# Reciprocals of attention denominators on 12 values a row, between two 32x32 block transpositions on VectorE

## The chip, the core and the metric

One core of a Trainium2 chip runs the whole program. It has TensorE (PE in the rows), VectorE (DVE), ScalarE (ACT), GpSimd (POOL) and SyncE (SP), and 16 DMA engines; each compute engine works off its own queue of instructions in order, and they meet at semaphores. The metric is the device time of one execution in microseconds (us).

## The reference

Three parts follow each other on 2304 tokens (4 batches of 576). The first is a linear attention with 8 heads of 64, whose result is divided, per token and head, by a denominator; the second a gated MLP (512 to 1536 to 512) behind an RMS norm; the third a soft mixture of 8 experts with 4 slots each. The change touches the division in the first part only.

```python
    q_p, k_p = (phi(q), phi(k))              # 256 features: exp(proj), exp(-proj)
    kv = np.einsum('bhsf,bhsd->bhfd', k_p, v)
    z = np.sum(k_p, axis=2)
    num = np.einsum('bhsf,bhfd->bhsd', q_p, kv)
    den = np.einsum('bhsf,bhf->bhs', q_p, z)[..., None] + 1e-06
    return (num / den).astype(np.float32)
    ...
    rms = np.sqrt(np.mean(x * x, axis=-1, keepdims=True) + 1e-06)
    xn = x / rms * rms_g
    g = xn @ w_gate
    silu = g * (1.0 / (1.0 + np.exp(-g)))
    return (silu * (xn @ w_val) @ w_out).astype(np.float32)
```

## The kernel before

The tokens are cut into 6 blocks of 384. The program has three stages, one behind the other in the text, but each engine's order of instructions is laid down when the program is built, by a planner that estimates when each operand is ready and prefers what stands earlier in the text; so work of neighbouring steps is interleaved.

The first stage (0 to 128 us of the trace) walks over 18 tiles of 128 tokens of k and v. In each iteration i it loads k for tile i+4 and v for tile i+2, projects k (L394), takes the largest magnitude and subtracts it (L398, L402 on VectorE), takes two exponentials (L415, L416 on ScalarE) and accumulates kv and z in PSUM (L439, L448). Beside that run the weights of the MLP, which come in 1 MB pieces and are converted in steps on ScalarE (L127, L129, L102), VectorE (the join, L137, L139) and GpSimd (L105), and the q side of block 0. The second stage (128 to 676 us) runs the MLP over the blocks 0 to 5: per block 12 steps m, in each the gate and value products (L806), an activation (L813, L814, L818), a split of the result in two parts (L102, L105) and the output products (L831 to L833). Beside block b of the MLP runs the q side of block b+1. The rest is the mixture's experts.

The q side of a block is four calls of attend(c), one for each pair of heads. Blocks 0 and 1 are of class Turned (features by projection, transposition and exponential, L339), blocks 2 to 5 of class Reduced (features by a maximum over partitions on GpSimd, L280). When the steps run is written out by hand: the lists TURNED0, TURNED1 and REDUCED give for each step the number of a slot; in block 0 two slots make one iteration i (3.5 us on average), in the MLP each m has three (2 to 3 us each).

attend(c) multiplies the features e of two heads with kv into num (L206, PSUM, 128 rows of head and dimension by 384 tokens) and with z into den (L214). For den the weight is one column spread to 32, so that each 32 rows of den hold the same denominators: rows 64*hh + 32*g to that + 31 hold head hh for the tokens of half g (192 each). ScalarE copies num out of PSUM (L216). VectorE adds 1e-6 to den (L218), takes reciprocals of all 128 x 192 (L219), and ScalarE spreads them by eight copies of 32 x 192 (L224) into the layout of num: rows of a head, both halves of the tokens. VectorE multiplies (L225), ScalarE squares (L228, L231), VectorE sums the squares of the four calls in s (L232). dn, the spread reciprocals and the squares are written into the e tiles, which come free with the last of them. After the call c = 3, scale() sums s over partitions on TensorE (ssq, L241), takes the inverse root on VectorE, and out() applies it (L254); then the block's values are split for the MLP (xnh, xnl). At the end of attend(3) of blocks 1 and 2, SP loads kv of a later batch (L236).

All loads are issued by SP, in one queue: k (raw, L385) and v (vt, L411), 256 KB each; weights (wraw, L123), 1 MB; q (qraw, L262 and L317), 192 KB; kv, 520 KB.

## Time and profile before

| | us |
|---|---|
| median of 3 runs | 742.65 (741.85 to 742.89) |
| span of the profiled execution, first to last instruction | 735.0 |
| median less that span | 7.65 |
| TensorE busy | 710.2 (97%) |
| VectorE busy | 429.5 (58%) |
| ScalarE busy | 371.8 (51%) |

Each row of a trace names the source line, the engine, the operation, the tile written and the tiles read with their shapes, how often, the busy time and the mean of one, and the idle time of that engine just before with the instruction that ended it. PEld is TensorE's loading of weights, which runs beside its products. Busy times of TensorE overlap a little, since its products are pipelined.

### The profile page before, as it was taken

To read this page: it belongs to the slowest core of one execution; us is meant where nothing else is said; L and a number is where in the kernel's file an instruction comes from. 1 tells how busy PE (TensorE), PEld (TensorE's weight loads), DVE (VectorE), ACT (ScalarE), POOL (GpSimd) and SP (SyncE) were. 2 spreads that over 40 slices of the span, in tenths; PEclk is the share of its full clock that TensorE was granted. 3 is DMA by queue.
4 is the path that set the end of the run, shared out by engine and by line. 5 is a ranking of instruction groups with operands and counts; after the bars stand their busy time and mean duration, and the time that the engine had idled before them with its cause. 6 is when DMAs were issued, how large, how long until landed. Compare 5 with 4: busy or idle time off the path is not lost.

```text
span 735.0 us, 12347 instructions
## 1 busy us (share of the span) xinstructions
PE 710.2 (97%) x4919; PEld 575.0 (78%) x4919; DVE 429.5 (58%) x808; ACT 371.8 (51%) x805; POOL 107.9 (15%) x60
## 2 busy tenths in 40 slices
PE   7998999999999999999999999999999999999895
PEld 4655555988889888898888989889888899988443
DVE  5998956798746556455565555655556453423313
ACT  6899855688445555345553456534465331211103
POOL 0232200234200211011210211201211010000100
PEclk9999999999999999999999999999999999999999
DMA  9683312544011010100010010000100137657898
GB/s 321 252 289 123 88 30 102 176 162 172 0 62 33 22 26 29 38 11 22 23 31 12 1 33 22 23 20 0 33 1 2 66 139 262 228 203 284 324 365 293
DMA packets 25145, 79.45 MB, mean 108 GB/s; under 512 B 2688, under 2 KB 13376, under 8 KB 18688
## 3 DMA queue, kind: packets, MB, share of 16 engines
q1 hardware_dynamic: 24864, 77.79, 30.2%
q10 hardware_dynamic: 224, 0.88, 0.4%
q8 instruction: 38, 0.62, 0.3%
q14 instruction: 19, 0.16, 0.1%
HBM read 71.99 MB, written 6.67 MB: 107 GB/s over the span
## 4 chain that ended last, share of the span: by engine, by line
PE 79%; DVE 9%; ACT 7%; issue 2%; POOL 1%; DMA 1%; SPq 0%; DVEq 0%; ACTq 0%; POOLq 0%
PE pv L806 20%; PE pg L806 19%; PE acc L831 6%; PE acc L832 6%; PE acc L833 6%; PE num L206 4%; PE kacc L439 2%; PE den L214 2%; ACT e L224 2%; PE y L945 2%; DVE wt L139 2%; PE y L961 2%; DVE wt L137 2%; PE P L394 1%; PE kacc L448 1%
## 5 line engine op out<-in xcount | busy, mean ns | idle before, releaser
L806 PE MATMUL pv<-xnh,wv 128*128 128x384 f32 x576 | 151.5, 344 | 0.0
L806 PE MATMUL pg<-xnh,wg 128*128 128x384 f32 x576 | 150.2, 342 | 0.6 <-DVE t L814 0.4
L806 PEld LDWEIGHTS pg<-xnh,wg 128*128 128x128 f32 x576 | 104.7, 188 | 6.3 <-ACT xnh L102 0.6
L806 PEld LDWEIGHTS pv<-xnh,wv 128*128 128x128 f32 x576 | 103.2, 188 | 7.0 <-issue 6.7
L806 PE MATMUL pv<-xnl,wv 128*128 128x384 f32 x288 | 97.7, 339 | 0.0
L806 PE MATMUL pg<-xnl,wg 128*128 128x384 f32 x288 | 97.5, 338 | 0.0
L831 PE MATMUL acc<-wo,hh 128*128 128x512 f32 x216 | 88.6, 410 | 0.0
L280 POOL PARTITION_ALL_REDUCE qe<-qe x32 | 50.0, 1563 | 262.5 <-ACT qe L279 242.8
L832 PE MATMUL acc<-wo,hh 128*128 128x512 f32 x216 | 85.8, 397 | 0.0
L833 PE MATMUL acc<-wo,hl 128*128 128x512 f32 x216 | 85.4, 396 | 0.0
L102 ACT CAST hh<-t 128x384 fp32r<-128x384 f32 x72 | 36.7, 510 | 80.6 <-PE acc L832 66.1
L105 DVE TENSOR_TENSOR hl<-t,hh 128x384 fp32r<-128x384 f32 x72 | 41.3, 574 | 51.2 <-ACT hh L102 48.6
L814 DVE SCALAR_TENSOR_TENSOR t<-t,pg 128x384 f32<-128x384 f32 x72 | 39.7, 551 | 51.8 <-ACT t L813 51.7
L813 ACT ACTIVATE t<-pg 128x384 f32<-128x384 f32 x72 | 35.2, 489 | 63.8 <-PE pg L806 63.7
L224 ACT COPY qe<-qe 32x192 f32<-32x192 f32 x128 | 44.8, 350 | 31.7 <-DVE qe L219 30.4
L818 DVE TENSOR_TENSOR t<-t,pv 128x384 f32<-128x384 f32 x72 | 39.7, 552 | 30.4 <-PE pv L806 29.3
L806 PEld LDWEIGHTS pg<-xnl,wg 128*128 128x128 f32 x288 | 54.0, 188 | 0.3 <-DVE xnl L105 0.3
L806 PEld LDWEIGHTS pv<-xnl,wv 128*128 128x128 f32 x288 | 54.1, 188 | 0.1
L833 PEld LDWEIGHTS acc<-wo,hl 128*128 128x128 f32 x216 | 40.6, 188 | 10.0 <-DVE hl L105 0.3
L831 PEld LDWEIGHTS acc<-wo,hh 128*128 128x128 f32 x216 | 40.7, 189 | 7.3 <-issue 0.3
L439 PE MATMUL kacc<-kp,vt 128*64 128x256 f32 (+1 forms) x320 | 44.8, 396 | 1.7 <-ACT kp L416 1.7
L832 PEld LDWEIGHTS acc<-wo,hh 128*128 128x128 f32 x216 | 40.7, 188 | 6.4
(187 smaller groups left out, 1065.5 us busy)
## 6 DMA issues: line engine op xcount, KB each, us to landing
eu<-in_w_dram SPq DMA_DIRECT2D x32, 1024.0 KB, 6.3
wraw<-in_wg_dram SPq DMA_DIRECT2D x6, 1024.0 KB, 5.0
wraw<-in_wv_dram SPq DMA_DIRECT2D x6, 1024.0 KB, 5.2
wraw<-in_wo_dram SPq DMA_DIRECT2D x6, 1024.0 KB, 4.8
qraw<-in_qT_dram SPq DMA_DIRECT2D x32, 192.0 KB, 2.3
raw<-in_kT_dram SPq DMA_DIRECT2D x18, 256.0 KB, 4.2
vt<-in_v_dram SPq DMA_DIRECT2D x18, 256.0 KB, 4.0
out_dram<-ob SPq DMA_DIRECT2D x18, 256.0 KB, 2.8
```

What stands on the lines that cost most here:

```text
L102: ACT.copy(out=hi, in_=src)
L105: (lo_eng or POOL).tensor_tensor(out=lo, in0=src, in1=hi.bitcast(F32), op=ALU.subtract)
L224: ACT.copy(out=rd[64 * hh + 32 * r:64 * hh + 32 * r + 32, g], in_=dn[o:o + 32])
L280: POOL.partition_all_reduce(e[:, 0], e[:, 1], channels=128, reduce_op=bass_isa.ReduceOp.absmax)
L439: PE.matmul(out=kva[o0:o0 + 64, hh // 2], lhsT=self.vt[r0:r1, h], rhs=kp[r0:r1, hh].rearrange("p s f -> p (s f)"), start=first and hh < 2, ...
L806: PE.matmul(out=p, lhsT=w[:, a, c], rhs=x, start=n == 0, stop=n == 11)
L813: ACT.activation(out=t, in_=g, func=AF.Tanh, scale=0.5)
L814: DVE.scalar_tensor_tensor(out=t, in0=t, scalar=1.0, in1=g, op0=ALU.add, op1=ALU.mult)
L818: DVE.tensor_tensor(out=t, in0=t, in1=wide("v", m, xs), op=ALU.mult)
L831: PE.matmul(out=acc[i], lhsT=hh[:, s], rhs=w[:, 0], start=m == 0, stop=False)
L832: PE.matmul(out=acc[i], lhsT=hh[:, s], rhs=w[:, 1], start=False, stop=False)
L833: PE.matmul(out=acc[i], lhsT=hl[:, s], rhs=w[:, 0], start=False, stop=m == MF - 1)
```

## The change

The reciprocals are taken on fewer values. Since each 32 rows of den hold the same 192 denominators, a transposition of 32x32 blocks by VectorE puts them one to a row: dt has, in row 32*q + j and block b, the denominator of token 32*b + j of that quarter, 32 times over; only its first column is used. rw gets these 6 values a row with 1e-6 added, in both of its two halves, and their reciprocals (12 values a row). Four transfers of 32 rows x 6 values (24 bytes a row), issued by SP, carry each quarter's values to the other quarter of the same head. A new step norm(c) then transposes rw, each value read 32 times, into rd (128 x 384), which is the layout of num, and multiplies; the squares and the sum s follow as before, with the squares in rd. The eight copies by ScalarE are gone, and the e tiles are last read by the products of den.

norm(c) is a step of its own in the lists: one slot behind attend(c) in blocks 0 and 1, two behind in blocks 2 to 5. The load of kv goes to a function next_kv(), called at the end of attend(3), behind the four transfers in the text. Three small tiles are new: dt (one buffer), rw (two), rd (one).

```diff
--- before.py
+++ after.py
@@ -189,7 +189,7 @@
 
         def __init__(self, sp, ps, blk, bufs):
             self.sp, self.ps, self.blk, self.bufs = sp, ps, blk, bufs
-            self.raw, self.x, self.e = {}, {}, {}
+            self.raw, self.x, self.e, self.rw = {}, {}, {}, {}
 
         def psum(self, name, shape):
             return self.ps.tile(shape, F32, tag="misc", name=name, bufs=self.bufs["misc"])
@@ -214,24 +214,37 @@
                     PE.matmul(out=den[o:o + 32], lhsT=kvt[b][:, 2 * c + hh, s, HD:HD + 1].to_broadcast([128, 32]),
                               rhs=e[hh][:, s, t:t + BLK // 2], start=s == 0, stop=s == 1, skip_group_check=True)
             ACT.copy(out=y, in_=num)
-            dn = e[0][:, 0, 0:BLK // 2]
-            DVE.tensor_scalar(out=dn, in0=den, scalar1=1e-6, scalar2=None, op0=ALU.add)
-            DVE.reciprocal(out=dn, in_=dn)
-            rd = e[1][:, 0].rearrange("p (g t) -> p g t", g=2)
+            nb = BLK // 64
+            dt = self.sp.tile([128, nb, 32], F32, tag="dt", name="dt", bufs=1)
+            DVE.transpose(out=dt.rearrange("p b j -> p (b j)"), in_=den)
+            self.rw[c] = rw = self.sp.tile([128, 2, nb], F32, tag="rw", name="rw", bufs=2)
+            DVE.tensor_scalar(out=rw, in0=dt[:, :, 0].rearrange("p (o b) -> p o b", o=1).to_broadcast([128, 2, nb]),
+                              scalar1=1e-6, scalar2=None, op0=ALU.add)
+            DVE.reciprocal(out=rw, in_=rw)
             for hh, g in halves:
                 o = 64 * hh + 32 * g
-                for r in range(2):
-                    ACT.copy(out=rd[64 * hh + 32 * r:64 * hh + 32 * r + 32, g], in_=dn[o:o + 32])
-            DVE.tensor_tensor(out=y, in0=y, in1=e[1][:, 0], op=ALU.mult)
+                to = 64 * hh + 32 * (1 - g)
+                SP.dma_start(out=rw[to:to + 32, g], in_=rw[o:o + 32, g])
+            if c == 3:
+                self.next_kv()
+
+        def norm(self, c):
+
+            y = xraw[self.blk][:, c]
+            rd = self.sp.tile([128, BLK], F32, tag="rd", name="rd", bufs=1)
+            rw = self.rw.pop(c).rearrange("p g (b o) -> p (g b) o", o=1)
+            DVE.transpose(out=rd.rearrange("p (b j) -> p b j", j=32), in_=rw.to_broadcast([128, BLK // 32, 32]))
+            DVE.tensor_tensor(out=y, in0=y, in1=rd, op=ALU.mult)
             if c == 0:
                 self.s = self.sp.tile([128, BLK], F32, tag="s", name="s", bufs=1)
                 ACT.activation(out=self.s, in_=y, func=AF.Square)
             else:
-                sq = e[1][:, 1]
-                ACT.activation(out=sq, in_=y, func=AF.Square)
-                DVE.tensor_tensor(out=self.s, in0=self.s, in1=sq, op=ALU.add)
+                ACT.activation(out=rd, in_=y, func=AF.Square)
+                DVE.tensor_tensor(out=self.s, in0=self.s, in1=rd, op=ALU.add)
+
+        def next_kv(self):
             for b, t0, t1 in block_parts(self.blk):
-                if c == 3 and self.blk * BLK + t1 == (b + 1) * SEQ and b + 2 < NB:
+                if self.blk * BLK + t1 == (b + 1) * SEQ and b + 2 < NB:
                     kvt[b + 2] = kvp.tile([128, NH, 2, HD + 1], F32, tag="kv", name=f"kv{b + 2}", bufs=2)
                     SP.dma_start(out=kvt[b + 2].rearrange("p h s d -> p (h s d)"), in_=kv_d[b + 2])
 
@@ -306,7 +319,8 @@
             a = [lambda c=c: self.attend(c) for c in range(4)]
             g = [lambda h=h: self.exps(h) for h in range(NH)]
             s = [first, *(x for c in range(4) for x in (f[2 * c], f[2 * c + 1], g[2 * c], g[2 * c + 1], a[c])), self.scale, self.out]
-            return sorted(zip(REDUCED, s), key=lambda x: x[0])
+            s = list(zip(REDUCED, s)) + [(REDUCED[5 * c + 5] + 2, lambda c=c: self.norm(c)) for c in range(4)]
+            return sorted(s, key=lambda x: x[0])
 
     class Turned(Q):
 
@@ -364,6 +378,7 @@
                     r.append((at[c] + i, lambda c=c, i=i: p(c, i)))
                     r.append((at[c] + i + lag, lambda c=c, i=i: self.turn(c, i, pr[c, i])))
                 r.append((attend[c], lambda c=c: self.attend(c)))
+                r.append((attend[c] + 1, lambda c=c: self.norm(c)))
             r += [(end[0], self.scale), (end[1], self.out)]
             return sorted(r, key=lambda x: x[0])
```

## Rows read from the trace of the kernel before

**Rows 1.** Busy time of each engine over the span (share) xinstructions, page, part 1

```profile
PE 710.2 (97%) x4919; PEld 575.0 (78%) x4919; DVE 429.5 (58%) x808; ACT 371.8 (51%) x805; POOL 107.9 (15%) x60
```

**Rows 2.** Stages: length, then busy us of each engine, granted TensorE clock, DMA share, GB/s

```profile
52.00:92.00 40.00, 37.12 (x369) 21.36 (x362) 35.84 (x53) 35.68 (x75) 11.86 (x5) 0.96 0.39 126
92.00:128.00 36.00, 34.85 (x345) 20.16 (x344) 21.74 (x49) 19.99 (x47) 0.00 (x0) 1.00 0.20 68
128.00:229.00 101.00, 98.62 (x597) 87.14 (x597) 75.64 (x122) 65.43 (x125) 23.07 (x9) 1.00 0.30 106
229.00:676.00 447.00, 445.86 (x2686) 392.75 (x2685) 235.19 (x473) 197.09 (x464) 60.06 (x36) 1.00 0.18 61
```

**Rows 3.** The same for the copies of L224 alone: ScalarE busy, count

```profile
52.00:92.00 40.00, 8.36 (x24) 0.96 0.39 126
128.00:229.00 101.00, 11.19 (x32) 1.00 0.30 106
229.00:676.00 447.00, 44.79 (x128) 1.00 0.18 61
```

**Rows 4.** Groups by line, 52 to 92 us: busy, mean ns | idle before, releaser

```profile
L224 ACT COPY e<-e 32x192 f32<-32x192 f32 x24 | 8.4, 348 | 1.6 <-DVE e L219 1.3
...
L219 DVE RECIPROCAL e<-e 128x192 f32<-128x192 f32 x3 | 4.0, 1350 | 0.1
...
L225 DVE TENSOR_TENSOR xraw<-xraw,e 128x384 f32<-128x384 f32 x3 | 1.7, 558 | 3.5 <-ACT e L224 3.5
...
L218 DVE TENSOR_SCALAR e<-den 128x192 f32<-128x192 f32 x3 | 1.0, 346 | 0.0
```

**Rows 5.** Waits of TensorE, 52 to 92 us: total us, times, longest

```profile
PE P L322 <- ACT xraw L216: 1.9, 1, 1.9
```

**Rows 6.** Lines 680 and 681, the mixture's own denominators: ns min/median/max

```profile
L680 DVE TENSOR_SCALAR cs<-cs x6: 168/168/169, 274.9 to 689.4; 128x3 f32<-128x3 f32 x6
...
L681 DVE RECIPROCAL cs<-cs x6: 176/176/176, 275.1 to 689.6; 128x3 f32<-128x3 f32 x6
```

**Rows 7.** SP's queue around the first call: start us, us, what

```profile
57.11 0.33 SPq L123 DMA_DIRECT2D wraw<-in_wo_dram  x1
57.53 0.38 SPq L385 DMA_DIRECT2D raw<-in_kT_dram  x1
58.48 0.33 SPq L411 DMA_DIRECT2D vt<-in_v_dram  x1
```

**Rows 8.** DMA issues, 0 to 20 us: KB each, median us to landing

```profile
wbd_f<-in_wbd_dram SPq DMA_DIRECT2D x1, 128.0 KB, 2.1
...
small<-in_rmsg_dram SPq DMA_DIRECT2D x1, 2.0 KB, 3.9
```

**Rows 9.** DMA issues, whole span

```profile
qraw<-in_qT_dram SPq DMA_DIRECT2D x32, 192.0 KB, 2.3
...
kv<-kv_d SPq DMA_DIRECT2D x2, 520.0 KB, 3.5
```

**Rows 10.** Waits of TensorE, 128 to 229 us, then 229 to 676 us

```profile
PE num L206 <- ACT e L339: 1.2, 1, 1.2
PE ssq L241 <- DVE s L232: 0.7, 1, 0.7
...
PE ssq L241 <- DVE s L232: 1.1, 4, 0.3
```

**Rows 11.** Timeline, VectorE and TensorE, end of block 2's q side

```profile
299.01 0.36 DVE L218 TENSOR_SCALAR qe<-den 128x192 f32<-128x192 f32 x1 [1.18 <-PE den L214]
...
304.26 0.56 DVE L225 TENSOR_TENSOR xraw<-xraw,qe 128x384 f32<-128x384 f32 x1 [2.15 <-ACT qe L224]
...
305.41 0.56 DVE L232 TENSOR_TENSOR s<-s,qe 128x384 f32<-128x384 f32 x1
...
306.02 0.83 PE L241 MATMUL ssq<-small,s 128*128 128x1 f32 x6 [0.29 <-DVE s L232]
```

**Rows 12.** SP's queue at the same place

```profile
299.00 0.33 SPq L236 DMA_DIRECT2D kv<-kv_d  x1
```

## The prediction, made before the change was run

> **What bounds the kernel now.** I read first the busy time of each engine over the span, then the same by stage, then the waits of the stages that leave an engine room. TensorE is busy for 710.2 of 735.0 us [rows 1], so a change on other engines is worth only what TensorE waits for them. The stages say where that is [rows 2]. From 229 to 676 us, where 16 of the 24 calls of attend() lie (blocks 2 to 5), TensorE is busy 445.86 of 447.00 us: nothing that leaves ScalarE there can shorten it by more than 1.1 us. From 128 to 229 us (block 1, 4 calls) it is busy 98.62 of 101.00 us: at most 2.4 us. From 92 to 128 us it is busy 34.85 of 36.00 us: at most 1.2 us. The stage with room is 52 to 92 us, with the first three calls of block 0: TensorE 37.12 of 40.00 us at a mean granted clock of 0.96, VectorE 35.84, ScalarE 35.68, all three near full and waiting for each other. TensorE's room there is 2.9 us of idle time and about 1.6 us (0.04 x 40) of clock, 4.5 us together.
>
> Next, what ScalarE does in that stage: 8.36 of its 35.68 us are the 24 spreading copies of L224 [rows 3]. They stall the others in two ways. VectorE waits 3.5 us for them at L225, of 4.2 us that it is idle in all [rows 4]; and the copy that empties num (L216) stands behind them on ScalarE, so that TensorE waits 1.9 us for a PSUM buffer [rows 5]. So the copies are on the path in this stage and beside the path everywhere else.
>
> **The change part by part.** Removed per call: eight copies on ScalarE, mean 348 ns, 2.9 us with their issue; on VectorE one addition over 192 columns (346 ns) and one reciprocal over 192 columns (1350 ns) [rows 4]. Added on VectorE: a transposition of 128x192 out of PSUM, an addition and a reciprocal over 12 columns, a transposition into 128x384; added on SP: four transfers of 32 x 24 bytes.
>
> The small ones have near rows: over 3 columns the same two operations took 168 and 176 ns [rows 6]. By the slope of the reciprocal, (1350 - 176) / 189 = 6.2 ns a column, 12 columns take 0.23 us; the addition 0.18 us. No row shows VectorE's transposition. Bounds: from nothing beyond a pass of the same size (L218 reads 128x192 of PSUM in 0.35 us, L225 passes 128x384 in 0.56 us [rows 4]) to twice that, if each element is handled twice; nothing in the trace makes it cheaper than a plain pass. I take the plain pass, 0.35 and 0.56 us, because both are one read and one write of those sizes. VectorE per call then: removed 0.35 + 1.35 = 1.70, added 0.35 + 0.18 + 0.23 + 0.56 = 1.32, so 0.4 us less; at the dear end 1.7 + 0.5, so 0.5 us more.
>
> The Trainium skill ("VectorE: DVE Perf Modes", "The three transpose paths") gives 311 ns for VectorE's transposition of 128x128 bf16, in 32x32 blocks; with one column a cycle of 0.96 GHz beyond that, an estimate from that page is 0.38 and 0.58 us, 0.05 us a call above the plain pass, some 0.2 us over the four calls of block 0, so 738.9 us in place of the forecast below. No row of before shows it.
>
> The transfers: SP issues two in a row 0.42 us apart (57.11, 57.53) [rows 7]; four take 1.3 us up to the last issue. How long so small a one takes no row shows in this stage. Nearest: 2 KB landed 3.9 us after issue between large loads, 128 KB 2.1 us as the first load of the program [rows 8], 192 KB 2.3 us in the median of the later stages [rows 9]. I take 2.2 us on a quiet queue and 3.9 us beside loads; a much lower end has no row, but a gain from it is only an earlier start of norm(), which waits for its slot anyway. From the end of the reciprocal to the end of the normalising product: now 2.9 + 0.6 = 3.5 us; after 1.3 + 2.2 + 0.56 + 0.56 = 4.6 us quiet, 6.3 us beside loads. But the reciprocal ends earlier by 1.70 - 0.76 = 0.94 us. So the product ends 0.2 us (quiet) to 1.9 us (beside loads) later than now.
>
> Whom the lateness meets: norm() is moved one slot (blocks 0 and 1) or two (2 to 5) behind attend(), 3.5 to 4 us of other VectorE work, so its transposition should mostly find the transfers landed, and the 3.5 us of stall at L225 should go. What is late next is VectorE itself and the weight join (L137, L139) on it. Behind the four transfers on SP stand loads of k, v and weights two iterations (18 of them fill 128 us, so 14 us) ahead of use; they wait for the reciprocal some microseconds longer, and I cost that at nothing; if that lead is gone, each call costs the landing of a load, about the 3.9 us of [rows 8]. The e tiles come free after the den matmuls instead of after L232; the trace shows nobody waiting for them.
>
> Sum by stage. 52 to 92 us: VectorE's floor is 40.0 - 4.2 - 3 x 0.4 = 34.6 us and TensorE's 35.5 us, so at most 4.5 us; the first call (57 us) issues behind a 1 MB and two 256 KB loads [rows 7], and its wait may even grow. I take 3.0 us (bounds -1 and 4.5). 92 to 128 us: the fourth call's sums end 0.2 us later, and TensorE idles 1.2 us in all: 0 (-1 to 1.2). 128 to 229 us: TensorE's two longest waits are 1.2 us for an exponential (ACT e L339) and 0.7 us for s at ssq [rows 10]; the first should go: 1.0 us (-2 to 2.4). 229 to 676 us: at each block's end TensorE already waits 0.3 us at the ssq matmuls, four times [rows 10]: in block 2 den's addition starts at 299.01, the product ends at 304.8, s is ready at 306.0 and ssq starts then [rows 11]. Quiet, this moves by +0.2 us: 0 in all (-4 to 1.1). Rest of the program: 0. Total 3.0 + 1.0 = 4.0 us less: span 731.0. The profiled span of 735.0 us lies 7.65 us below the median of the runs, 742.65; with that unchanged, 738.7 us.
>
> **The rivals.** First: ScalarE was only one of three full engines. VectorE at 34.6 of 40 us, in an order laid down before the run, takes the stall back elsewhere; or the transpositions cost twice. Then 52 to 92 us gives 0.5 us and the rest nothing: 742.1 us. For it: VectorE and TensorE are 90 and 93% busy there. Against: the 1.9 and 3.5 us waits name ScalarE.
>
> Second, slower: the transfers come late and TensorE waits at each block's end for s. The place is ssq (L241), in blocks 1 to 5. SP issues in block 1 and 2 also a load of kv, 520 KB, 3.5 us to landing [rows 9], that needs only the den matmuls (299.00 us [rows 12]) and so can get in front of the four transfers; then they land like the 2 KB among loads, and s comes 1.9 us later. Five ends x 1.9 = 9.5 us, less the 4.0: 748.2 us if at all five; with 1.9 at the two with kv and 0.5 at the other three, 5.3 less 4.0, 744.0 us. It decides from 0.8 us of lateness a block on (5 x 0.8 = 4.0). For it: TensorE has no margin at ssq. Against: three of the five ends have DMA nearly idle (0.18 mean share [rows 2]), and the order of ssq on TensorE can be later than now.
> The Trainium skill ("DMA: Bandwidth & Descriptors", "Queues, rings and completion order") says that each DMA engine consumes what one issuing engine queued in ring order, which speaks for this rival: a small transfer does not pass SP's load. [...] The 3.9 us for 2 KB agree.
>
> Third, better: every wait goes, 4.5 + 1.2 + 2.4 + 1.1 = 9.2 us: 733.5 us. Against it, VectorE's floor.
>
> **How the numbers follow.** Forecast 0.50 (736.5 to 741), first rival 0.22, second 0.16, third 0.12. About 0.2%, 1.5 us, is what a measurement of this kernel can tell from no change, so "same" is 741.2 to 744.1. Faster: 0.50 + 0.12, less 0.02 of the forecast's slow edge, 0.60. Same: 0.22 + 0.02 = 0.24. Slower: 0.16. The range reaches from 733.5 (third rival) to 745.5, which holds the second rival where only some block ends are late; out of it are its dear half and the bounds taken all at once. Predicted is the forecast's 738.7.
>
> **What would show it.** Right: L224 gone; ScalarE's busy time 64 us less over the three stages of [rows 3]; VectorE's idle time ahead of norm()'s transposition under 1.5 us in 52 to 92 us; TensorE's wait for L216 gone and its clock there at 1.00; the first gate matmul of block 0, which now starts as the third stage of [rows 2] begins, 2 to 4 us earlier; block length from 229 us on unchanged. Wrong: the four transfers landing over 3 us after issue with VectorE idle before norm(); ssq waiting over 0.8 us in each block; transpositions over 0.7 us; or that matmul no earlier, with VectorE's idle time merely moved.

## The result and the profile after

The changed kernel took 744.03 us (median of 13 runs) beside 741.87 us for the kernel before (13 runs): ratio 1.0053, 95% interval 1.0027 to 1.0078. The ratio goes by the means, 745.00 and 741.09 us; the two medians alone would give 1.0029. Measured a second time, it was 1.0058 (1.0036 to 1.0080). So it is 0.5% slower, 3.9 us in the means; 738.7 us and "faster" were predicted. Ratios are of fast runs; one execution of no_transfers_edge (1396 us) was slow and is left out.

The profiled execution spans 741.2 us, 6.2 more than that of before, and that is more than the change cost. Wherever the time and the span of an execution are both on record, the time is 1.7 to 3.5 us above the span. The trace of before, with 735.0 us, is therefore of one of its fastest executions: other spans of that kernel go from 734.9 to 742.1 us, with medians of 737.4 to 738.6 on three chips.

Busy time over the span, and the stages (length, then busy us of TensorE, weight loads, VectorE, ScalarE, GpSimd, granted clock, DMA share, GB/s), beside [rows 1, 2]:

```profile
PE 714.1 (96%) x4919; PEld 574.7 (78%) x4919; DVE 428.5 (58%) x856; ACT 304.4 (41%) x613; POOL 108.9 (15%) x60
```

```profile
52.00:92.00 40.00, 36.03 (x328) 20.68 (x326) 33.57 (x50) 26.92 (x48) 12.18 (x5) 0.91 0.37 117
92.00:128.00 36.00, 35.03 (x366) 19.96 (x368) 24.69 (x58) 16.47 (x35) 0.00 (x0) 1.00 0.21 70
128.00:229.00 101.00, 97.19 (x601) 84.50 (x592) 75.60 (x125) 53.09 (x93) 21.84 (x9) 1.00 0.31 109
229.00:676.00 447.00, 446.66 (x2684) 391.41 (x2683) 232.42 (x511) 153.81 (x340) 61.87 (x36) 1.00 0.17 59
```

The copies [rows 3, 4] are gone and ScalarE has 67.4 us less to do. VectorE has nearly as much as before (428.5 against 429.5). The granted clock of 52 to 92 us, which was to rise from 0.96 to 1.00, fell to 0.91.

The new operations of VectorE (count, then busy us, mean ns, idle before and its releaser):

```profile
L236 DVE STREAM_TRANSPOSE rd<-rw 128x384 f32<-128x384 f32 x24 | 13.8, 575 | 17.9 <-DMA rw<-rw 17.9
L237 DVE TENSOR_TENSOR xraw<-xraw,rd 128x384 f32<-128x384 f32 x24 | 13.6, 566 | 0.9
L219 DVE STREAM_TRANSPOSE dt<-den 128x192 f32<-128x192 f32 x24 | 9.1, 380 | 23.6 <-PE den L214 23.6
L221 DVE TENSOR_SCALAR rw<-dt 128x12 f32<-128x12 f32 x24 | 6.1, 254 | 0.6
L223 DVE RECIPROCAL rw<-rw 128x12 f32<-128x12 f32 x24 | 5.4, 226 | 0.7
```

The four operations that replace the addition and the reciprocal sum to 34.4 us (L236, L219, L221, L223); the two old ones took 24 x (0.35 + 1.35) = 40.8. The 6.4 us saved were taken back by others: the subtraction hl<-t,hh (L105, 72 times) rose from 41.3 to 46.6 us in all, since three of them, beside a subtraction on GpSimd, took 2.4 to 2.8 us in place of 0.56, and the sum s (18 times) rose from 10.0 to 14.3.

The transfers: from issue to landing (KB each, median us), then the time that SP takes to issue one (ns min/median/max):

```profile
rw<-rw SPq DMA_DIRECT2D x96, 0.8 KB, 1.7
```

```profile
L227 SPq DMA_DIRECT2D rw<-rw x96: 507/583/1350, 59.2 to 587.0; - x96
```

TensorE's waits, 52 to 92 us and then 128 to 229 us (total, times, longest), beside [rows 5, 10]: the wait for the copy of num, 1.9 before, grew, and new ones stand in the MLP's first block.

```profile
PE P L336 <- ACT xraw L216: 2.7, 1, 2.7
...
PE acc L848 <- DVE hl L105: 1.8, 2, 1.0
PE pg L821 <- DVE t L829: 1.7, 1, 1.7
```

**Where the 6.2 us between the two traces lie.** Three marks in each trace cut the program: the first gate product of the MLP, the first copy of block 1's outputs (L869, L884 after), two blocks on, and that of block 4's, three whole blocks later. "Tail" is from there to the end of the span.

| us | first gate product | from there to outputs of block 1 | three blocks | tail | span | ratio to before (95%) |
|---|---|---|---|---|---|---|
| before | 128.05 | 194.46 | 279.99 | 132.5 | 735.0 | 1 |
| after | 130.78 | 196.21 | 280.30 | 133.9 | 741.2 | 1.0053 (1.0027–1.0078) |
| after_again | 134.22 | 196.23 | 280.30 | 133.6 | 744.3 | 1.0058 (1.0036–1.0080) |
| copies_out | 133.54 | 194.40 | 278.35 | 133.0 | 739.3 | 1.0071 (1.0044–1.0099) |
| copies_out_h13 | 132.02 | 196.10 | 278.35 | 133.0 | 739.5 | 1.0055 (1.0033–1.0077) |
| copies_back | 131.07 | 197.67 | 280.64 | 136.8 | 746.2 | 1.0062 (1.0036–1.0088) |
| copies_kept | 127.54 | 197.97 | 278.43 | 135.6 | 739.5 | 1.0049 (1.0031–1.0068) |
| no_transfers | 126.45 | 194.13 | 278.34 | 136.3 | 735.2 | 0.9976 (0.9956–0.9996) |
| no_transfers_h13 | 129.63 | 194.11 | 278.34 | 136.9 | 739.0 | 0.9972 (0.9951–0.9993) |
| no_transfers_edge | 126.24 | 194.27 | 278.34 | 132.8 | 731.6 | 0.9944 (0.9924–0.9964) |
| held13 | 126.13 | 195.78 | 280.49 | 132.9 | 735.3 | 1.0001 (0.9977–1.0025) |
| held13_join | 127.32 | 194.50 | 280.45 | 135.5 | 737.8 | 1.0001 (0.9986–1.0016) |
| two_queues | 132.04 | 195.98 | 279.12 | 132.5 | 739.6 | 1.0055 (1.0033–1.0077) |
| held13_2q | 126.83 | 195.97 | 279.65 | 132.6 | 735.0 | 0.9990 (0.9968–1.0012) |
| join_2q | 132.51 | 193.89 | 279.09 | 134.1 | 739.6 | 1.0024 (1.0000–1.0047) |
| held13_join_2q | 126.47 | 193.91 | 279.09 | 132.5 | 732.0 | 0.9961 (0.9942–0.9981) |
| all_three_again | 126.56 | 193.93 | 279.11 | 132.4 | 732.0 | 0.9963 (0.9938–0.9988) |
| before_join | 133.56 | 194.16 | 280.02 | 132.5 | 740.2 | 1.0008 (0.9992–1.0023) |

After against before: +2.7 up to the MLP, +1.8 in its first two blocks, +0.3 in the three blocks, +1.4 in the tail. Two warnings on reading this. The middle columns repeat within 0.02 us where one kernel was traced twice (after and after_again; no_transfers and no_transfers_h13); the first column moves by 3.4 us between after and after_again, and by 5.5 us between before and before_join, whose order is the same up to that mark (128.05 and 133.56), because TensorE's waits and its clock differ from one execution to the next. So whether after lies behind before there is not shown by these two traces: the 3.9 us in the means, less the 2.1 of the two middle columns, leave an estimate of 1.8 us for the first column and the tail together. And the tail has two lengths: 132.4 to 133.6 us, or 133.9 to 136.9 where the clock falls near 690 us. So the middle columns may be read from one trace; the first column and the tail need several traces and the ratios beside them.

### The profile page after: what moved, and what is told of

Read it like the earlier page. It is cut to its first block, busy times and chain, and to the rows that moved or that the text cites. A ratio compares the mean times of both kernels' runs of the same rounds, so it can differ in the third digit from the quotient of the medians.

```text
span 741.2 us, 12309 instructions
## 1 busy us (share of the span) xinstructions
PE 714.1 (96%) x4919; PEld 574.7 (78%) x4919; DVE 428.5 (58%) x856; ACT 304.4 (41%) x613; POOL 108.9 (15%) x60
## 4 chain that ended last, share of the span: by engine, by line
PE 82%; DVE 9%; ACT 3%; DMA 2%; issue 1%; POOL 1%; SPq 0%; DVEq 0%; ACTq 0%
PE pv L821 19%; PE pg L821 18%; PE acc L848 6%; PE acc L846 6%; PE acc L847 6%; PE num L206 4%; PE kacc L454 4%; DVE wt L137 3%; PE den L214 2%; PE y L960 2%; PE P L409 2%; PE kacc L463 2%; DVE wt L139 2%; PE y L976 2%; DMA wraw<-in_wg_dram 1%
## 5 line engine op out<-in xcount | busy, mean ns | idle before, releaser
L105 DVE TENSOR_TENSOR hl<-t,hh 128x384 fp32r<-128x384 f32 x72 | 46.6, 647 | 58.0 <-ACT hh L102 53.1
L829 DVE SCALAR_TENSOR_TENSOR t<-t,pg 128x384 f32<-128x384 f32 x72 | 39.6, 551 | 48.2 <-ACT t L828 48.2
L298 ACT ACTIVATE qe<-qe 128x384 f32<-128x384 f32 x32 | 16.8, 526 | 49.9 <-DVE qe L297 49.9
```

The lines of the kernel that those rows point to most:

```text
L105: (lo_eng or POOL).tensor_tensor(out=lo, in0=src, in1=hi.bitcast(F32), op=ALU.subtract)
L829: DVE.scalar_tensor_tensor(out=t, in0=t, scalar=1.0, in1=g, op0=ALU.add, op1=ALU.mult)
```

## The experiments

### What is the relief of ScalarE worth by itself?

copies_out is the kernel before without the eight copies (the product reads the reciprocals in place, so the division is left out in part). copies_back is the changed kernel with eight copies that nobody reads.

```diff
-                for r in range(2):
-                    ACT.copy(out=rd[64 * hh + 32 * r:64 * hh + 32 * r + 32, g], in_=dn[o:o + 32])
-            DVE.tensor_tensor(out=y, in0=y, in1=e[1][:, 0], op=ALU.mult)
+            DVE.tensor_tensor(out=y, in0=y, in1=e[0][:, 0], op=ALU.mult)
```

> The kernel before, with the eight spreading copies of L224 left out and nothing in their place (the product at L225 takes its second factor from the tile of the reciprocals, so the division is wrong; all else is as before, the long reciprocals too). It shows what ScalarE's freed 67 us are worth by themselves. Order theory (what the copies' going changes is the order that the planner lays down, and ScalarE's new idle time goes into waits for GpSimd and for weight loads): within 2 us of the kernel before, 740 to 744 us, and 52 to 92 us no shorter by more than 1 us. Transfer theory (the relief is worth the 3 to 5 us that the prediction gave it, and the four transfers with their waits eat it): 737 to 739 us.

> The changed kernel with the eight copies of 32x192 put back on ScalarE behind the first transposition, into the tile where they went before; nobody reads them. If ScalarE's time were worth anything, this would be 3 us or more slower than the changed kernel, 747 us or more. Order theory: the planner sorts the weight steps behind the copies again, as in the kernel before, and the time is the changed kernel's or better, 741 to 745 us, with TensorE's wait for the num copy under 2 us.

Less work made the kernel slower (1.0071), outside the range of either theory, and the copies put back cost the changed kernel nothing that the ratios can tell (1.0062 beside 1.0053). In copies_back TensorE's wait for the copy of num is gone, as the order theory had it, but TensorE waits 3.3 us for another result of ScalarE (kvs) in its place, and the column to block 1's outputs is 1.5 us longer. So no gain from freeing ScalarE shows in the first 130 us. Each of the two edits also gives a new order, so the price of ScalarE's time at a fixed order is not shown. And copies_out's three blocks are 1.64 us shorter than those of before, 0.55 us a block: there the relief does shorten the path, where the prediction expected nothing.

### One edge of order

When the program is built, the planner lays down each engine's order. What it did with the freed time of ScalarE, from 57 us (start, us, engine, line, and in brackets the idle time before with its releaser), and the product of TensorE that waits:

```profile
57.39 1.05 ACT L102 CAST wo<-wt 128x1024 fp32r<-128x1024 f32 x1 [0.59 <-DVE wt L139]
58.35 1.20 ACT L129 ACTIVATE wraw<-wraw 128x1024 uint32<-128x1024 uint32 x1
61.27 1.20 ACT L127 ACTIVATE wt<-wraw 128x1024 f32<-128x1024 f32 x1 [1.73 <-POOL wo L105]
...
64.44 1.05 ACT L102 CAST wg<-wt 128x1024 fp32r<-128x1024 f32 x1
65.37 0.49 ACT L216 COPY xraw<-num 128x384 f32<-128x384 f32 x1
```

```profile
65.92 1.22 PE L336 MATMUL P<-wbd_f,qraw 128*128 128x256 f32 x2 [2.66 <-ACT xraw L216]
```

The place of the copies is taken by a weight piece from a later iteration (L127 at 61.27). Its buffer comes free only with GpSimd's subtraction, so ScalarE stands still 1.73 us with the four exponentials kp and the copy of num behind it. In held13 that piece, the one of iteration 13, is issued behind the copy of num, where it stands in the kernel before:

```diff
-            ACT.copy(out=y, in_=num)
+            numcopy[self.blk, c] = ACT.copy(out=y, in_=num).ins
...
+HOLD = {13: 1}
...
+                    if i in HOLD:
+                        with tc.issue_after(numcopy[0, HOLD[i]]):
+                            conv_scale()
```

> The changed kernel with one edge of order more: the scaling of the weight piece of iteration 13 (two instructions on ScalarE) is queued behind the copy of num of attend(1) of block 0, where it stands in the kernel before; in the changed kernel it stands ahead of four exponentials and that copy, and waits 1.7 us for GpSimd. Order theory: TensorE's wait of 2.7 us before 66 us shrinks under 1 us, its clock from 64 to 76 us stays above 0.9, and the first gate matmul comes 2 to 4 us earlier than 130.8, so 740 to 742 us. Transfer theory: unchanged, 743 to 745 us.

```profile
61.06 0.63 ACT L432 ACTIVATE kp<-pr 128x512 f32<-128x512 f32 x1 [2.50 <-DVE pr L419]
...
64.09 0.47 ACT L218 COPY xraw<-num 128x384 f32<-128x384 f32 x1
64.46 1.16 ACT L128 ACTIVATE wt<-wraw 128x1024 f32<-128x1024 f32 x1
```

The copy of num comes 1.28 us earlier, but that alone did not end the wait. TensorE's product at the same place in held13:

```profile
63.70 0.67 PE L338 MATMUL P<-wbd_f,qraw 128*128 128x256 f32 x2 [1.03 <-DVE qpr L342]
```

It starts before the copy of num (64.09): in the new order another of VectorE's results (qpr) releases it, after 1.03 us. So the edge works through the whole order laid down anew. And the wait had cost more than its length. Windows of 4 us in before, after and held13, in this order (the granted clock is the third number from the end):

```profile
64.00:68.00 4.00, 3.35 (x22) 2.33 (x24) 4.00 (x8) 4.00 (x6) 1.36 (x1) 0.73 0.07 5
68.00:72.00 4.00, 4.00 (x36) 2.14 (x33) 2.29 (x5) 3.90 (x11) 1.02 (x1) 0.84 0.32 118
```

```profile
64.00:68.00 4.00, 2.08 (x10) 1.44 (x11) 2.40 (x7) 2.94 (x6) 2.36 (x1) 0.68 0.18 68
68.00:72.00 4.00, 4.00 (x22) 2.13 (x18) 2.30 (x5) 2.84 (x5) 0.00 (x0) 0.50 0.27 66
```

```profile
64.00:68.00 4.00, 4.00 (x50) 2.45 (x48) 4.00 (x8) 4.00 (x6) 2.73 (x1) 1.00 0.23 86
68.00:72.00 4.00, 3.47 (x36) 2.47 (x30) 4.00 (x7) 4.00 (x9) 0.00 (x0) 1.00 0.19 34
```

Behind the wait of 2.66 us the clock stood at its lower level, 1.2 GHz, through 68 to 72 us; before it was back sooner; in held13, with no such wait, it never left 2.4 GHz, and the first gate product came 4.65 us earlier than in after. (It is 1.92 us earlier than in before and 7.4 earlier than in before_join, so against before one trace says little.) In all five traces with this edge on the changed kernel that product is at 126.1 to 127.3 us, in the four without it (after, after_again, two_queues, join_2q) at 130.8 to 134.2, each with a wait for the copy of num of 2.6 to 2.9 us. The edge constrains one piece; the planner lays what follows anew, so what is shown is that the same instructions in another order win back the loss, not that this one wait is all of it.

copies_out_h13, the same edge on copies_out, shows the limit.

> The kernel before without its 32 copies for the denominators (the product of line 225 reads the 192 reciprocals in place, so the output is scaled wrongly), and with one edge of order: the weight piece scaled in iteration 13 of the first stage is issued on ScalarE behind the copy of num of the second attend, where it stands in the kernel before. Without the edge this kernel took 1.0071 [1.0044, 1.0099] of before. If the loss came from where that piece lands in ScalarE's queue, the edge takes it back and the relief shows: 735 to 740 us, ratio 0.990 to 0.999, no wait of TensorE of over 1 us for the copy of num in 52-92 us. If removing work from ScalarE costs in another way (the order of other steps, or VectorE's product being met by other work), it stays at 1.004 to 1.008.

It stayed at 1.0055, within the interval of copies_out. In its trace another pair met, which was not tested by itself: VectorE's product L222 took 1.82 us beside GpSimd's subtraction, 0.56 in before, ahead of the differences that ScalarE's exponentials wait for, and TensorE still waited 1.7 us for the copies of num. The edge is no cure for every version; each has its own order with its own collisions.

### VectorE's part alone

copies_kept is the kernel before with the transpositions and the few reciprocals, but ScalarE's copies, no transfers and no step norm().

```diff
-            DVE.tensor_scalar(out=dn, in0=den, scalar1=1e-6, scalar2=None, op0=ALU.add)
-            DVE.reciprocal(out=dn, in_=dn)
+            DVE.transpose(out=dt.rearrange("p b j -> p (b j)"), in_=den)
+            DVE.tensor_scalar(out=rw, in0=dt[:, :, 0:1], scalar1=1e-6, scalar2=None, op0=ALU.add)
+            DVE.reciprocal(out=rw, in_=rw)
+            DVE.transpose(out=dn.rearrange("p (b j) -> p b j", j=32), in_=rw.to_broadcast([128, nb, 32]))
```

> The kernel before with VectorE's part of the change alone: transposition, 12 or so values of addition and reciprocal, transposition back into the 192 values, then the 8 copies of ScalarE and the product as they were; no transfers, no step of its own. VectorE's part by the durations of the changed kernel is 0.38 + 0.17 + 0.23 + about 0.4 in place of 0.35 + 1.34 = 0.5 us less per call, ahead of the same copies. If less work on a path that TensorE waits for is worth its time: 739 to 741, ratio 0.995 to 0.999. If what the planner lays down around it decides, the sign is open: anything from 0.994 to 1.006, and the two orders differ around 60 us.

1.0049: slower, with 0.5 us a call less on VectorE by the durations and as much on ScalarE. The three blocks gained 1.56 us; between the first gate product and block 1's outputs it lost 3.5, and the tail's clock fell. A second version with less work in sum loses as much as the change.

### The transfers

no_transfers is the changed kernel without its four transfers (half the rows keep the other half's reciprocals).

```diff
-                to = 64 * hh + 32 * (1 - g)
-                SP.dma_start(out=rw[to:to + 32, g], in_=rw[o:o + 32, g])
```

> The changed kernel with the four transfers of a call left out (half of the rows then hold the other half's reciprocals, so the division is wrong). Transfer theory: 4 to 6 us faster than the changed kernel, 738 to 740 us, since VectorE no longer waits 17.9 us for them and SP's 2.4 us a call are gone. Order theory: no gain that follows from the transfers, 741 to 746 us, with TensorE's wait for the num copy (2.7 us in the changed kernel) still there if the weight step still stands ahead of that copy on ScalarE.

It measured 0.9976, 0.8% (5.7 us) below after. The size is what the transfer theory gave, and outside the order theory's 741 to 746 us; the wait for the copy of num stayed (2.7 us at the longest), as the order theory said. So both are true in part. Without the transfers, and with the order that the planner then lays down, the three blocks are 1.96 us shorter than in after and the stretch to block 1's outputs 2.08, in both traces of this kernel. Under the label no_transfers_h13 the same kernel ran once more: the edge of which its expectation speaks was not in it, so the expectation has no answer there, and 0.9972 is a repeat.

> The changed kernel without its four small transfers for each group of heads (half of the rows keep the wrong half's reciprocals), with the same edge of order. Without the edge it took 0.9976 [0.9956, 0.9996]. The predicted gain (4 us, of which 3.0 in 52-92 us) had no price on the transfers' issue nor on the order: if order and transfers are the two losses, this one is at 0.990 to 0.995, with TensorE's wait for the copy of num gone and the first gate matmul at 125 us or earlier. If the edge does nothing here (its first 3.3 us of waits only move to other steps), 0.996 to 0.999.

The version with the edge ran later:

> The changed kernel without its small transfers (half of the rows keep the wrong half's reciprocals), with the edge of the weight piece of iteration 13 behind the second copy of num; the run labelled no_transfers_h13 was the kernel without that edge, a repeat of no_transfers. By the order theory the wait for the copy of num (2.7 to 4.0 us in the two traces without the edge) goes, the clock stays at 1.00 in 60 to 76 us, and the time falls from 0.9974 to 0.991 to 0.995 (732 to 735 us). If the edge only moves the wait to another step, 0.996 to 0.999.

0.9944, in the range that the order theory gave, and the wait for the copy of num is gone from TensorE's waits. So the edge is worth 0.3% without the transfers and 0.5 to 0.6% with them (held13 beside after and after_again). In the three blocks the transfers cost 1.96 us (280.30 against 278.34), 0.65 us a block. Where, the weight loads of TensorE show, which wait ahead of the products (229 to 676 us; before, after, two_queues in this order: total, times, longest):

```profile
PEld ssq L241 <- DVE s L232: 2.4, 4, 0.6
```

```profile
PEld pg L821 <- DVE xnl L105: 1.6, 4, 0.4
...
PEld pg L821 <- issue: 1.1, 4, 0.3
PEld ssq L254 <- DVE s L243: 0.8, 4, 0.2
```

```profile
PEld ssq L254 <- DVE s L243: 1.2, 4, 0.3
```

Before lost 0.6 us at the ssq products of each block. After, these are laid into the middle of the value products and wait 0.2; but the normalisation ends later, and the next block's first gate product waits for its input (xnl). no_transfers has neither wait. The end of block 2 in after, to be held against [rows 11, 12]:

```profile
303.37 0.33 SPq L249 DMA_DIRECT2D kv<-kv_d  x1
303.38 0.38 DVE L219 STREAM_TRANSPOSE dt<-den 128x192 f32<-128x192 f32 x1 [1.18 <-PE den L214]
304.48 0.23 DVE L223 RECIPROCAL rw<-rw 128x12 f32<-128x12 f32 x1
304.74 2.42 SPq L227 DMA_DIRECT2D rw<-rw  x4
308.40 0.56 DVE L105 TENSOR_TENSOR hl<-t,hh 128x384 fp32r<-128x384 f32 x1 [1.91 <-ACT hh L102]
308.87 0.57 DVE L236 STREAM_TRANSPOSE rd<-rw 128x384 f32<-128x384 f32 x1
309.48 0.56 DVE L237 TENSOR_TENSOR xraw<-xraw,rd 128x384 f32<-128x384 f32 x1
310.63 0.56 DVE L243 TENSOR_TENSOR s<-s,rd 128x384 f32<-128x384 f32 x1 [0.59 <-ACT rd L242]
311.24 0.83 PE L254 MATMUL ssq<-small,s 128*128 128x1 f32 x6
```

SP needs 2.42 us for four issues, and kv does stand in front of them. It cost nothing there: the last of the four lands 3.57 us after the reciprocal, and in the blocks from 3 on, with no kv, that is 3.5 to 3.8 us in ten calls of twelve. The path is four issues and one landing. The product ends 6.66 us after VectorE first reads den (309.48 + 0.56 - 303.38), 5.81 before [rows 11]. two_queues issues two of the four on ScalarE's queue, from block 2 on:

```diff
-                SP.dma_start(out=rw[to:to + 32, g], in_=rw[o:o + 32, g])
+                (ACT if hh and self.blk > 1 else SP).dma_start(out=rw[to:to + 32, g], in_=rw[o:o + 32, g])
```

> The changed kernel, but in the reduced blocks (from 229 us) two of the four small transfers of a group of heads are issued on ScalarE's queue and two on SP's; the first 229 us are laid down as in the changed kernel. In its trace a block from 327 us on is 93.4 us; without transfers it is 92.8 and in the kernel before 93.3. If the time that SP needs for four issues (2.4 us for the four) delays the last group's product so far that the next block's first gate waits for its split input, halving the issue shortens each of these blocks by 0.4 to 0.6 us: sum of the three blocks from the second to the fifth copy of the outputs 278.4 to 279.2 us in place of 280.3, and 1.5 to 2.5 us in all (742 us, ratio 1.001 to 1.004). If the landing of the transfers or the step's slot sets it, the blocks stay at 93.4 and the ratio at 1.005.

The three blocks shortened by 1.18 us, as expected, and the gate's wait is gone. The ratio, expected at 1.001 to 1.004, showed nothing of it (1.0055): a gain of 1 to 2 us lies inside the interval, 3.3 us wide, while the first 130 us still had their loss.

The Trainium skill ("DMA: Bandwidth & Descriptors", "Rules for kernel authors") says that spreading transfers over issuing engines saves only the issuing time. The rows agree: the ones on ScalarE's queue landed 2.0 us after issue, no sooner than SP's 1.7 in after. But the last of four landed about 2.6 us after the reciprocal where it was 3.6, and on this chain the issuing time is what counts.

### The joins in the MLP's first block, and the three together

After, around 183 us, GpSimd, VectorE and the TensorE product that waits:

```profile
182.10 2.64 POOL L105 TENSOR_TENSOR wg<-wt,wg 128x1024 fp32r<-128x1024 f32 x1 [3.64 <-ACT wg L102]
183.15 2.68 DVE L137 SCALAR_TENSOR_TENSOR wt<-wt,wraw 128x1024 uint32<-128x1024 uint32 x1 [0.32 <-issue]
185.75 0.54 DVE L829 SCALAR_TENSOR_TENSOR t<-t,pg 128x384 f32<-128x384 f32 x1
186.34 0.62 PE L821 MATMUL pg<-xnh,wg 128*128 128x384 f32 x2 [1.68 <-DVE t L829]
```

A join, 1.21 us when alone, takes 2.68 beside GpSimd's subtraction and stands in front of the gate's step, for which TensorE waits. held13_join issues each join of that block behind the gate's step (L829) that stands ahead of it in the text, tgate[0]:

```diff
-                        conv_join()
+                        with tc.issue_after(tgate[0]):
+                            conv_join()
```

> The changed kernel with the edge of held13 (1.0001 [0.9977, 1.0025]) and one more: in the first block of the MLP each join of a weight piece on VectorE is issued behind the gate's VectorE step that stands before it in the program, so that a join of 1.2 us, which GpSimd's subtraction stretches to 2.4, can no longer stand in front of that step. If the 2 us that block 0 of the MLP lost to before (TensorE waits 1.8 us for t at line 829) come from that order, the time falls to 736.5 to 739, ratio 0.994 to 0.998. If the late weight loads set it (ScalarE waits 1.2 to 2.5 us for them), the joins only come later and it stays at 0.999 to 1.004.

> The changed kernel with all three repairs: the edge of the weight piece of iteration 13, the joins of the MLP's first block behind the gate's step, and two queues for the transfers in the reduced blocks. The three losses read from the traces are 2.7 us (52-92 us), 1.3 of 1.8 us (first MLP block) and 0.5 a block; if they add, the steady blocks are at 92.8 to 93.0, the first gate matmul at 126 to 127.5 us, and the time is 736 to 738 us, ratio 0.994 to 0.998, faster than both kernels. If they don't add because the clock falls elsewhere instead (in the first 130 us or at 690 us), it stays at 0.999 to 1.002.

> The kernel before with the one edge of held13_join that it doesn't have already: the joins of the first MLP block behind the gate's step. (The other edge, of iteration 13, is there in its order anyway.) In its trace TensorE waits only 0.4 us for t in that block, so if the edge repairs what the change upset, it is worth nothing here: ratio 0.998 to 1.002. If it is an improvement whatever the kernel, 0.995 to 0.998, and what held13_join_2q gains on before would be partly this.

held13_join did what it should in the trace (195.78 to 194.50 us) and nothing in the ratio (1.0001 both); its profiled execution had the clock fall at 690 us, where held13's had not. It also speaks on the late weight loads: ScalarE still waits 8.6 us for them in that block (11.3 in held13), and yet the loss is gone. All three repairs together: 0.9961, faster than both kernels. On the kernel before the joins' edge is worth nothing (1.0008), and the other edge is its order already, so these two edges are no gain by themselves on the kernel before. Four versions side by side on one chip test whether the losses add:

> The changed kernel itself, as the reference on the same chip as the three others: 1.003 to 1.008 of before, as in its first measurement (1.0053 [1.0027, 1.0078]).

> The changed kernel with the edge of iteration 13 and the two queues, without the edge of the joins. If the three losses add and the joins' is 1.3 us as in the traces of held13 and held13_join, it takes 1 to 2 us more than all_three_again (0.9975 to 0.9995 of before). If the joins' edge is worth nothing to the medians (held13 1.0001 and held13_join 1.0001), it equals all_three_again within 0.1%.

> The changed kernel with the joins' edge and the two queues, without the edge of iteration 13: the wait for the copy of num and the clock's fall behind it stay (2.7 us by the trace). If the edge of iteration 13 is the largest of the three, 1.001 to 1.004 of before, with the first gate matmul at 130 to 132 us; if the other two carried the gain, 0.996 to 0.999.

> The kernel of held13_join_2q once more (0.9961 [0.9942, 0.9981] then): 0.994 to 0.998 of before, and 0.7 to 1.2% below after_again on the same chip, if the three losses that the traces show are the loss of the change and its gain lies under them.

The ratios came out in the ranges given: 1.0058 without repair, 1.0024 without the edge of iteration 13, 0.9990 without the joins', 0.9963 with all (join_2q's first gate product, at 132.5 us, lies past its 130 to 132). By these and held13_join, the edge of iteration 13 is worth 0.61% (4.5 us), the joins' 0.27% (2.0 us), the two queues 0.38% (2.8 us). Their sum, 9.3 us, is more than the 7.0 measured directly between after_again and all_three_again (about 2 us of uncertainty), and other pairs give other shares: 0.57% for the first edge (after_again, held13), 0.00 or 0.31% for the joins (held13 and held13_join; two_queues and join_2q), 0.00 or 0.11% for the queues (after and two_queues; held13 and held13_2q). So the ratios show that the three together are worth 0.95%, most of it the edge of iteration 13; the shares of the other two are shown by the columns alone, 1.3 to 2.1 us for the joins and 0.8 to 1.4 for the queues in the three blocks.

**The tail.** In after and held13 TensorE has the same waits from 680 us on, to 0.01 us, and yet the clock fell in after; the first products behind them (after, then held13):

```profile
692.41 1.08 PE L786 MATMUL stp<-G,S_run 96*128 96x32 f32 x8 [0.19 <-DVE S_run L783]
693.92 5.11 PE L960 MATMUL y<-eu,xo 128*32 128x512 f32 x32 [0.43 <-DVE xo L787]
```

```profile
687.51 1.08 PE L792 MATMUL stp<-G,S_run 96*128 96x32 f32 x8 [0.19 <-DVE S_run L789]
689.03 3.64 PE L966 MATMUL y<-eu,xo 128*32 128x512 f32 x32 [0.44 <-DVE xo L793]
```

1.47 us more for 32 products, in part at the lower level. after_again had no such fall, so this part of the 6.2 us belongs to the one execution, not to the change; its tail is nevertheless 1.1 us longer than that of before. What decides either stays open.

## Why the prediction was wrong

**Costs of the operations: right.** VectorE per call was put at 1.32 us; measured 0.38 + 0.17 (median; the mean is 0.25) + 0.23 + 0.58 = 1.36. The estimate for the transpositions from the Trainium skill's 311 ns ("VectorE: DVE Perf Modes", "The three transpose paths"), 0.38 and 0.58, is what the trace has (0.380 and 0.575); the plain pass was a little cheap. ScalarE lost 64.4 us over the three stages, as forecast. The transfers' path came out right by two errors that cancel: four issues take 0.58 us each, not 0.42, and landing 1.7 us, not 2.2 (1.8 + 1.7 = 3.5, forecast 1.3 + 2.2). That norm() "should mostly find the transfers landed" was wrong: 15 of 24 transpositions waited for them, 17.9 us in all, most of it in the blocks from 229 us on.

**"With that unchanged", the 7.65 us between span and median: a wrong reading.** No execution on record has over 3.5 us between its time and its span, after has 1.9. The 735.0 us are of one short execution, set beside the median of others. The 4.0 us of gain do not rest on it, but the rows of before come from an execution that was faster than most.

**52 to 92 us, "3.0 us less": this step failed.** It took the waits that name ScalarE (1.9 and 3.5 us) as the worth of ScalarE's time, and reckoned with the order as it was. The stall at L225 did go: VectorE is idle 0.0 us ahead of norm()'s transposition in that stage, under the 1.5 of the list. But the planner filled the time with other work that had to wait itself, the copy of num came no earlier (65.37 against 64.14), and the wait grew to 2.7 us, with the clock behind it; in all four traces of this order it is 2.6 to 2.9 us, in the two of before's order 1.9 and 1.3. In place of 3.0 us less, the four have the first gate product at 130.8 to 134.2 us, the two of before's order at 128.05 and 133.56; by the estimate above, the loss there and in the tail is 1.8 us. held13 shows that the same work can run without that wait and at a clock of 1.00, but not by the mechanism forecast: there the copy of num comes at 64.09, as in before, and the product of TensorE no longer waits for it. That its first gate product is 1.9 us earlier than in before, near the "2 to 4 us" of the list, is one trace against one.

**128 to 229 us, "1.0 us less": wrong too.** From the first gate product to the outputs of block 1, two blocks on, it is 1.75 us more, 1.5 of it before the second block's first gate product. The wait for the exponential went, as predicted; waits for the gate's step (1.7) and for hl (1.8) came. With joins and queues repaired the same stretch is 0.5 us less than before.

**229 to 676 us, "0": right in sum, wrong in both parts.** The block length is unchanged (93.43 against 93.33 us). But "at most 1.1 us" was read from the idle time of TensorE's products, where the waits at ssq show 0.3 us each [rows 10]; its weight loads show 0.6, and copies_out, copies_kept and no_transfers all win 0.55 us a block. The transfers took it back. The second rival is near to what happened: the last product came 0.85 us later in block 2, between "0.2 quiet" and "1.9 beside loads" and just past its breaking point of 0.8. But the load of kv was not the cause: blocks without one are as long (93.4 to 93.5 us). The price was not paid at ssq either, since TensorE had it moved behind part of the value products (the point held against this rival), but at the next block's first gate product, and it was 0.65 us a block.

**"An order laid down before the run takes the stall back elsewhere"**, the first rival, was the right mechanism, priced as if it could at worst eat the gain (742.1). It can overshoot: by the ratios the new order lost 4.5 us (about 2 us of uncertainty) against the same kernel with one edge, more than the 3.0 that was to be gained. That the weight loads come later on SP was costed at nothing; ScalarE waited up to 2.5 us for them in the MLP's first block, but with the joins moved most of that waiting stays and TensorE's loss is gone, so the joins' place decided there.

The forecast's size was not far off for what the edit can give: with all three repairs it is 0.37% below before, 2.7 us, and without the transfers (and with half of the rows wrong) 0.56%, 4.1 us, against 4.0 forecast. That nearness is luck in part: of the 4.1 us, 1.65 lie in the three blocks from 322 us on, where the forecast had none, and 0.2 in the two blocks before, where it had 1.0.

## What to carry to other kernels

Where a planner orders the queues, an edit changes two things, the work and the order; price the second with both signs, and hold the old order with an edge to see the first by itself. A wait that names an engine says that its instruction came late, not that its time is what was short: look at what will fill the gap, and what that in turn waits for. Lengths between marks that repeat to 0.02 us separate losses that medians with 2 us of spread cannot. Hold the span of a profiled execution against those of other runs before two traces are subtracted: one of the two may be among the fastest of its kernel.

## What the runs showed of the hardware

- A VectorE instruction can last as long as the GpSimd subtraction beside it: the join 2.68 us in place of 1.21, the product 1.82 in place of 0.56, the 12-column addition up to 1.93 in place of 0.17. Before's gate step (L814), which reads one operand from PSUM, kept its 0.54 in the two cases beside it, and before's reciprocal over 192 columns its 1.35 in five. The Trainium skill ("SBUF — State Buffer", "SBUF: two separate sides") describes an exclusive lock between these two engines for VectorE instructions with two SBUF inputs or in a two-port mode; the rows agree, with the join ending 1.1 us after GpSimd's instruction. The 12-column addition has one input; whether it ran in such a mode, no row shows.
- Behind one wait of 2.66 us TensorE's clock stood at 1.2 GHz through 68 to 72 us and for part of 64 to 68, which is 3.3 us of full speed by the rows (4 x 0.32 + 4 x 0.50), more than the wait itself; near 690 us the clock fell behind the same waits in one execution and not in the other.
- A transfer of 32 rows x 24 bytes inside SBUF lands 1.7 us after its issue, but SP is occupied 0.58 us by each, 0.33 by a load of 1 MB. In after, 33 of the 96 were issued while an earlier load of SP was under way, and none landed before it.
